# GT = X^T phi(K) in five pieces of 512 columns and a turned strip of 128, with the last two head groups of kv formed later

## The chip, the cores and the metric

One core of one Trainium2 chip runs the whole kernel. The metric is the device time of one execution in microseconds; before the change its median over three runs is 724.76 us (724.48 to 725.0). The kernel's products run on TensorE (PE in the profile, PEld for its weight loads), sums and low halves on VectorE (DVE), copies, high halves and activations on ScalarE (ACT); SyncE (SP) and GpSimd (POOL) issue nearly all DMAs.

## The reference

The input x has 2048 rows of 640. A linear attention block with 32 heads of 20 and a gated linear unit of width 1536 are mixed by a gate:

```python
qkv = x @ wqkv                      # q, k, v: 32 heads of 20
phi = lambda t: where(t > 0, t + 1, exp(t)) + 1e-6
kv  = einsum("bhsd,bhse->bhde", phi(k), v)
z   = einsum("bhsd->bhd", phi(k))
o   = einsum("bhqd,bhde->bhqe", phi(q), kv) / (einsum("bhqd,bhd->bhq", phi(q), z) + 1e-6)
a   = o @ wo
b   = (sigmoid(x @ w_gate) * (x @ w_up)) @ w_down
g   = sigmoid((x * gate_w).sum(-1))
out = g * a + (1 - g) * b
```

All in float32.

## The kernel before

**Precision.** A product in float32 is made of three in a faster format (fp32r): each operand is split into a high and a low half, and `mm3` (lines 406 to 412) issues high x high, high x low and low x high. The split itself (`split`, line 437) is a copy on ScalarE for the high half and a subtraction on VectorE for the low half; names end in h and l. So an operand is ready for its second product only when VectorE has made its low half.

**Stage 1, GT.** V is never formed. Instead the kernel sums GT = X^T phi(K), 640 x 640, over the 16 token tiles of 128 (`GTBatch`, line 978), in five batches: of 2 tiles, three of 4, and 2. A batch has ten pieces, u = 0 to 9: piece u = 2m + h is the block of 128 rows m and of 320 columns h. Each piece gathers its tiles in one PSUM bank (three products a tile) and is then added to `gt` in SBUF by VectorE (in the first batch, copied, some of them by ScalarE). The stationary operand is a block of 128 columns of x (XN), the moving one 320 columns of phi(K) (PK). Between the batches stand the K projections of the next tokens. The eight PSUM banks have four names, ch, dd, cc and rot, with two banks each in turn. Lines 1161 to 1195 run batches 1 to 3, lines 1197 to 1210 the last one (`glast`); its last four sums are put off to the start of the next stage (`p1_tail`).

**Stage 2, the q phase.** `q_phase` (line 2178) has 16 steps for the second half of the tokens: j = 0 and 1 are steps 1 and 2 of a block A (units 2 and 3 of q by a scheme with seven products, s1 to s7), j = 2 and 3 two whole units of q, j = 4 and 5 steps 1 and 2 of a block B (units 0 and 1), j = 6 to 10 steps 3 to 7 of A, j = 11 to 15 those of B. In step 2 of a block VectorE adds the bank dd to c11, in step 5 ScalarE copies ch to c22 and VectorE adds cc to it. Between the steps a table of lists, `extra[j]` (lines 2430 to 2444), puts the small products of the attention, head group by head group (six groups, called parts 0 to 5 below, of 120, 120 and four times 100 columns):

- `kv_part` (line 1573) multiplies a part's columns of `gt` with wv (five plain float32 products, line 1578), and VectorE masks the result to the heads' blocks and splits it (kvt, kvh, kvl). Parts 0 to 5 stand at j = 1, 1, 3, 6, 6, 8.
- `m_part` (line 1589) multiplies a part's kvh, kvl with woh, wol, the halves of that part's rows of wo: two banks, three products of 320 columns each; the second and fifth product read wol. ScalarE copies the results out (ms). Parts 0 to 5 stand at j = 5, 6, 8, 10, 12, 13. The split of wo (`wo_split`, line 1561) is queued two parts ahead; it frees a tile for the load of a further part.

**What sets the order.** Every engine runs its instructions in the order in which the program lists them. The class `Order` makes this list: it keeps a clock for TensorE, ScalarE and VectorE by rough costs, and one for the DMA queues, and `fill` (line 116) puts queued work (splits, sums) on ScalarE and VectorE when by these clocks it is ready and does not make them late. `need(key)` (line 189) puts a queued item at once, ready or not, because a product that reads it comes next. A queued split of wo counts as ready when its load has landed by the planner's clock (line 1571). After stage 1 that clock of SyncE's queue is set forward to the last landing of a DMA that GpSimd issued:

```python
    sp.t = max(sp.t, gp.cell[0])          # line 1508
    load_w()
```

and behind it stand the loads of the raw weights (`wst`), of wv and of wo. `sp.t` and `gp.cell` belong to the planner alone; no instruction comes of them.

Of the kernel before, what the change touches and what calls it, by code (L numbers as in the profile page):

```python
# [7 lines left out]
F32 = mybir.dt.float32  # L8
F32R = mybir.dt.float32r
AF = mybir.ActivationFunctionType  # L10
# [360 lines left out]
def v_cost(w):  # L371
    return 0.07 + w / 960

@with_exitstack
def gated_mix_kernel(ctx: ExitStack, tc: tile.TileContext, xt, xn, wk, wv, wo, wst_q, wst_f, out_t):
# [30 lines left out]
    def mm3(out, l_hi, l_lo, r_hi, r_lo, first, last):  # L406
        nc.tensor.matmul(out, l_hi, r_hi, start=first, stop=False, skip_group_check=True)  # L407
        nc.tensor.matmul(out, l_hi, r_lo, start=False, stop=False, skip_group_check=True)  # L408
        nc.tensor.matmul(out, l_lo, r_hi, start=False, stop=last, skip_group_check=True)  # L409
# [8 lines left out]
    def act(out, src, fn, after="", **kw):  # L418
        order.on_act(width(out), after, out, src)
        nc.scalar.activation(out, src, fn, **kw)  # L420
# [44 lines left out]
    fac_dram = dram.tile([P, NG, P], F32, name="fac_dram")  # L465
    z_dram = dram.tile([P // H, H, DH], F32, name="z_dram")
    m_dram = dram.tile([D, D], F32, name="m_dram")
    mr_dram = dram.tile([P, KC, D], F32, name="mr_dram")
    bdn = HPG * DH

# [12 lines left out]
    def m1_tile(tag, name, dt=F32, rows=P):  # L483
        return m1.tile([rows, D], dt, name=name, tag=tag, bufs=2 if tag == "ma" else 3)
# [489 lines left out]
    def queue_split(b):  # L974
        for s in range(2):
            order.add(a_cost(D), v_cost(D), lambda s=s: k_split(tok(b, s)), ("pk", b))

    class GTBatch:
        def __init__(self, n, blocks):
            self.n, self.tiles = n, [tok(b, s) for b in blocks for s in range(2)]  # L980
            self.ps = {}

        def part(self, u, t0, t1, tag="rot", out=True):
            m, h = divmod(u, 2)
            cs = slice(h * HALF, (h + 1) * HALF)
            ms = slice(m * P, (m + 1) * P)
            if u not in self.ps:
                self.ps[u] = ps_tile(tag)
            ps = self.ps[u][:, :HALF]
            for n in range(t0, t1):  # L990
                i = self.tiles[n]
                mm3(ps, XN[i][0][:, ms], XN[i][1][:, ms], PK[i][0][:, cs], PK[i][1][:, cs],
                    n == 0, n == len(self.tiles) - 1)
            if t1 == len(self.tiles) and out:
                self.out(u)

        def out(self, u):
            m, h = divmod(u, 2)
            ps, dst = self.ps[u][:, :HALF], gt[:, m, h * HALF:(h + 1) * HALF]
            if self.n == 0 and u < 4:  # L1000
# [78 lines left out]
    queue_xn(1)  # L1079
    g = GTBatch(0, [0])  # L1080
    order.slack(True)
    for u in range(2 * KC):
        g.part(u, 0, 2, "rot" if u % 2 else "dd")
        order.fill()
    order.slack(False)
# [2 lines left out]
    for c in range(1, 4):  # L1088
        ck = chunks[c]
        if c == 1:  # L1090
            queue_qw(2)
        a, b = KBlock(2 * c), KBlock(2 * c + 1)
        for n in range(1, 6):
            order.need((ck, n))
            if c == 1 and n >= 3:
                order.need(("ks", (1, 0, 2)[n - 3]))
            getattr(a, f"s{n}")()
            getattr(b, f"s{n}")()
            for _ in range(({1: 1, 2: 1, 3: 1, 5: 1}, {3: 2, 4: 2, 5: 2})[c - 2].get(n, 0) if c > 1 else 0):
# [12 lines left out]
        a.s6()  # L1112
        a.s7()
        a.sum_b()
        a.phi_a()
        b.s6()
        a.phi_b()
        order.need(("pk", 2 * c - 1))
        k_split(tok(2 * c, 0))
        b.s7()  # L1120
        b.sum_b()
        k_split(tok(2 * c, 1))
        if c == 3:
# [46 lines left out]
        for u in range(6 if c == 1 else 4):  # L1170
            g.part(u, 0, 2, ("rot", "dd", "ch", "cc")[u % 4])
# [16 lines left out]
        for u in range(2 * KC):  # L1188
            g.part(u, 2 if u in g.ps else 0, len(g.tiles),
                   ("rot", "dd", "rot", "cc")[u % 4] if c == 3 or u < 8 else "rot")  # L1190
            order.fill()
            if u in (3, 5, 7, 9,):
                order.run("qw")
            if c == 2 and u == 9:
                queue_ls()
    order.need(("xn", 7))
    glast = GTBatch(4, [7])
    tags = ["rot", "rot", "ch", "ch", "dd", "dd", "cc", "cc", "rot", "rot"]

    for u in range(4):  # L1200
        glast.part(u, 0, 2, tags[u])
    for u in range(4, 10):
        glast.part(u, 0, 2, tags[u], out=False)
        order.fill()
        if u == 5:
            wg_split(("q", 1, KC - 1), w_stage)
        elif u == 8:
            glast.out(4)
            glast.out(5)
    p1_tail = [lambda u=u: glast.out(u) for u in range(6, 10)]  # L1210
    p1_cm.__exit__(None, None, None)

    pw_cm = tc.tile_pool(name="pw", bufs=1, side="right", reuse_waits="tile")
# [1793 lines left out]
```

## Time and profile before

| | |
|---|---|
| median of three runs | 724.76 us |
| the profiled execution: span from the first to the last instruction | 722.5 us |
| TensorE busy, share of the span | 718.2 us, 99% |
| VectorE, ScalarE, GpSimd busy | 587.1, 370.0, 114.0 us |
| granted TensorE clock | 1.000 |
| stage 1, last GT product to the q phase | 140.99 us from the span's start |
| products of GT | 480, of 320 columns |

The profile gives the span of one execution and not its own time on the clock of the runs; the median lies 2.26 us above the span. A line of a timeline gives start, duration, engine, line of the program, operation, what it writes and reads, and the shapes; in brackets stand the idle time of the engine before it and what ended it. TensorE's products are pipelined: their durations overlap, and the time that one takes in a stream is the distance from start to start.

### The profile page before, as it was taken

How to read it: one execution, taken by the hardware profiler on the slowest of the kernel's cores; microseconds unless marked ns; L12 is line 12 of the kernel's file. 1: busy time of each engine (PE TensorE's matmuls, PEld its weight loads, DVE VectorE, ACT ScalarE, POOL GpSimd, SP SyncE). 2: the span in 40 equal slices, each digit the busy share in tenths (PEclk: the TensorE clock that was granted, in tenths of full speed). 3: DMA queues.
4: the chain of work that ended last, by engine and by line, in shares of the span. 5: the costliest groups of instructions: out<-in, count | busy, mean ns of one | idle time of the engine just before them, and what ended most of it. 6: DMA issues, size and time to landing. Idle time of an engine off the chain costs nothing.

```text
span 722.5 us, 10190 instructions
## 1 busy us (share of the span) xinstructions
PE 718.2 (99%) x3539; PEld 616.7 (85%) x3539; DVE 587.1 (81%) x1028; ACT 370.0 (51%) x686; POOL 114.0 (16%) x184
## 2 busy tenths in 40 slices
PE   9999999999999999999999999999999999999998
PEld 8999999988888888888888888888888888888886
DVE  6898888988677989898989977447696968799895
ACT  6884748367556654545364664354423242454451
POOL 0211112113311212111210224001010101002200
PEclk9999999999999999999999999999999999999999
DMA  7677689598787866757687899968989895959947
GB/s 258 162 230 182 179 196 286 129 357 280 273 303 259 325 241 234 262 221 264 244 321 273 255 313 360 404 222 292 364 256 309 247 395 182 407 217 332 217 101 240
DMA packets 81690, 191.31 MB, mean 265 GB/s; under 512 B 12154, under 2 KB 40202, under 8 KB 77926
## 3 DMA queue, kind: packets, MB, share of 16 engines
q1 hardware_dynamic: 60726, 117.72, 49.6%
q0 software_dynamic: 20624, 72.70, 30.2%
q8 instruction: 28, 0.46, 0.3%
q10 hardware_dynamic: 288, 0.23, 0.1%
q14 instruction: 24, 0.20, 0.1%
HBM read 113.14 MB, written 75.20 MB: 261 GB/s over the span
## 4 chain that ended last, share of the span: by engine, by line
PE 99%; DMA 0%; DVE 0%; ACT 0%; issue 0%
PE ch L407 11%; PE ch L409 11%; PE ch L408 11%; PE cc L409 9%; PE cc L407 9%; PE cc L408 9%; PE dd L407 7%; PE dd L408 7%; PE dd L409 7%; PE rot L407 5%; PE rot L408 5%; PE rot L409 5%; PE rot L1578 1%; PE dd L2735 1%; PE ch L2735 0%; DMA xnh<-wk 0%
## 5 line engine op out<-in xcount | busy, mean ns | idle before, releaser
L420 ACT ACTIVATE c<-ch 128x512 f32<-128x512 f32 x54 | 32.3, 597 | 84.2 <-PE ch L409 83.4
L424 DVE TENSOR_TENSOR hf<-c,hf 128x512 fp32r<-128x512 f32 x80 | 54.4, 687 | 19.3 <-ACT hf L420 18.9
L420 ACT ACTIVATE hf<-c 128x512 fp32r<-128x512 f32 x80 | 48.9, 624 | 31.1 <-DVE c L424 31.0
L424 DVE TENSOR_TENSOR c<-cc,c 128x512 f32<-128x512 f32 x42 | 28.9, 688 | 28.3 <-PE cc L409 17.4
L407 PE MATMUL ch<-xth,ws 128*128 128x512 f32 x112 | 43.6, 389 | 0.0
L408 PE MATMUL ch<-xtl,ws 128*128 128x512 f32 x112 | 43.6, 389 | 0.0
L409 PE MATMUL ch<-xth,ws 128*128 128x512 f32 x112 | 43.6, 389 | 0.0
L424 DVE TENSOR_TENSOR c<-c,c 128x512 f32<-128x512 f32 x52 | 35.7, 687 | 3.3 <-ACT c L420 2.7
L424 DVE TENSOR_TENSOR tb<-rot,tb 128x512 f32<-128x512 f32 x56 | 36.1, 682 | 0.3 <-PE rot L409 0.3
L407 PE MATMUL dd<-xrh,wg 128*128 128x512 f32 x90 | 35.2, 391 | 0.0
L408 PE MATMUL dd<-xrl,wg 128*128 128x512 f32 x90 | 35.1, 390 | 0.0
L409 PE MATMUL dd<-xrh,wg 128*128 128x512 f32 x90 | 35.0, 389 | 0.0
L420 ACT ACTIVATE c<-dd 128x512 f32<-128x512 f32 x22 | 13.1, 596 | 41.4 <-PE dd L409 41.4
L407 PE MATMUL cc<-xbh,ws 128*128 128x512 f32 x84 | 32.7, 389 | 0.0
L408 PE MATMUL cc<-xbl,ws 128*128 128x512 f32 x84 | 32.7, 389 | 0.0
L409 PE MATMUL cc<-xbh,ws 128*128 128x512 f32 x84 | 32.7, 389 | 0.0
L424 DVE TENSOR_TENSOR tb<-dd,tb 128x512 f32<-128x512 f32 x36 | 24.7, 686 | 9.3 <-PE dd L409 9.2
L420 ACT ACTIVATE dd<-ch 128x512 f32<-128x512 f32 x22 | 12.8, 582 | 35.9 <-PE ch L409 35.9
L424 DVE TENSOR_TENSOR tb<-cc,tb 128x512 f32<-128x512 f32 x36 | 24.5, 684 | 1.9 <-PE cc L409 1.9
L424 DVE TENSOR_TENSOR wst<-wst 128x256 f32<-128x256 f32 (+1 forms) x65 | 24.6, 396 | 1.4
L409 PEld LDWEIGHTS ch<-xth,ws 128*128 128x128 f32 x112 | 21.0, 188 | 4.7 <-DVE ws L424 0.3
L408 PEld LDWEIGHTS ch<-xtl,ws 128*128 128x128 f32 x112 | 21.0, 188 | 4.3
(703 smaller groups left out, 2378.9 us busy)
## 6 DMA issues: line engine op xcount, KB each, us to landing
wf<-ws POOLq DMA_DIRECT2D x12, 1152.0 KB, 7.5
ws<-wf SPq DMA_DIRECT2D x11, 1152.0 KB, 8.8
wst<-wst_f SPq DMA_DIRECT2D x12, 640.0 KB, 4.9
wf<-wg POOLq DMA_DIRECT2D x12, 640.0 KB, 6.1
wd<-wd POOLq DMA_DIRECT2D x12, 640.0 KB, 8.1
wg<-wf SPq DMA_DIRECT2D x12, 640.0 KB, 6.9
wf<-wd SPq DMA_DIRECT2D x10, 640.0 KB, 11.0
xnst<-xn SPq DMA_DIRECT2D x16, 320.0 KB, 4.5
```

Source lines behind the costliest of these rows:

```text
L407: nc.tensor.matmul(out, l_hi, r_hi, start=first, stop=False, skip_group_check=True)
L408: nc.tensor.matmul(out, l_hi, r_lo, start=False, stop=False, skip_group_check=True)
L409: nc.tensor.matmul(out, l_lo, r_hi, start=False, stop=last, skip_group_check=True)
L420: nc.scalar.activation(out, src, fn, **kw)
L424: nc.vector.tensor_tensor(out, a, b, op=op)
L1578: nc.tensor.matmul(ps[:w, :w], v[:, m, :w], gt[:, m, c0:c0 + w], start=(m == 0), stop=(m == KC - 1))
L2735: nc.tensor.matmul(ps, l, r, start=new, stop=j == 1 and k == ks[-1], skip_group_check=True)
```

## The change

A GT batch now has seven pieces instead of ten. Pieces 0 to 4 hold 128 rows of GT each and its first 512 columns: the same stationary operands, 512 moving columns. The last 128 columns of GT are made transposed: now the 128 columns of PK are stationary and x moves, in two pieces of 384 and 256 columns (`STRIP`). They gather in the same place of `gt`, columns 512 to 640, but there element (r, m, c) is GT's element (m 128 + c, 512 + r). In the last batch the two strip pieces come first; then VectorE transposes the strip within blocks of 32 x 32 into a tile `turned`, GpSimd's queue stores it in DRAM and fetches it back in four DMAs with the blocks exchanged, and ScalarE copies it into `gt` (`gt_back`, at the end of step j = 8). Head groups 4 and 5 reach into these columns; their kv parts move from j = 6 and 8 to j = 9 and 10. `GTBatch.part`, `out` and the loops over pieces follow; lines from 986 on are shifted by 30 in the end.

```diff
+    STRIP = {KC: (0, 3), KC + 1: (3, KC)}
+    def gt_turn():
+        turned = m1_tile("mb", "turned")
+        order.on_vec(D, "", 1.0, turned, gt[:, :, TG:])
+        nc.vector.transpose(turned.rearrange("p (b m c) -> p m b c", m=KC, c=H),
+                            gt[:, :, TG:].rearrange("p m (b c) -> p m b c", c=H))
+        gp.dma_start(gt_dram, turned)
+        back = m1_tile("mb", "back")
+        src = gt_dram.rearrange("(a r) (b n) -> b r a n", r=H, b=P // H)
+        for b in range(P // H):
+            gp.dma_start(back[b * H:(b + 1) * H].rearrange("r (a n) -> r a n", a=P // H), src[b])
+        BACK.append(back)
+    def gt_back():
+        act(gt[:, :, TG:].rearrange("p m (a c) -> p a m c", c=H),
+            BACK[0].rearrange("p (a m c) -> p a m c", m=KC, c=H), AF.Copy)
...
-            ps = self.ps[u][:, :HALF]
             for n in range(t0, t1):
-                i = self.tiles[n]
-                mm3(ps, XN[i][0][:, ms], XN[i][1][:, ms], PK[i][0][:, cs], PK[i][1][:, cs],
-                    n == 0, n == len(self.tiles) - 1)
+                x, pk = XN[self.tiles[n]], PK[self.tiles[n]]
+                if u < KC:
+                    ms = slice(u * P, (u + 1) * P)
+                    ps, l, r = self.ps[u], [t[:, ms] for t in x], [t[:, :TG] for t in pk]
+                else:
+                    b0, b1 = STRIP[u]
+                    ps = self.ps[u][:, :(b1 - b0) * P]
+                    l, r = [t[:, TG:D] for t in pk], [t[:, b0 * P:b1 * P] for t in x]
+                mm3(ps, *l, *r, n == 0, n == len(self.tiles) - 1)
...
-    for u in range(4):
+    for u in (KC, KC + 1, 0):
         glast.part(u, 0, 2, tags[u])
-    for u in range(4, 10):
+    order.add(0, v_cost(D), gt_turn, "turned", first=True)
+    for u in range(1, KC):
         glast.part(u, 0, 2, tags[u], out=False)
         order.fill()
...
-    for hg, (j, t) in enumerate(((1, "rot"), (1, "rot"), (3, "cc"), (6, "rot"), (6, "rot"), (8, "rot"))):
+    for hg, (j, t) in enumerate(((1, "rot"), (1, "rot"), (3, "cc"), (6, "rot"), (9, "rot"), (10, "rot"))):
         extra[j].append(lambda hg=hg, t=t: kv_part(hg, t))
+    extra[8].append(gt_back)
```

The planner then lists the work of VectorE and ScalarE in another order. Numbers behind a name tell buffers apart. VectorE in the q phase before, from the low half of wo's part 1 (wol_1966; that of part 0 stands earlier) to the sum of block B's step 2 (c11_2003):

```order
L424 TENSOR_TENSOR wol_1966<-wo_sb_1841,woh_1965 120x640
L424 TENSOR_TENSOR xz_1528<-xz_1528 128x512
L424 TENSOR_TENSOR xtl_1521<-xst_89,xth_1520 128x2x256
L424 TENSOR_TENSOR xtl_1521<-xz_1528,xth_1520 128x2x256
L424 TENSOR_TENSOR kvt_1984<-cc0_1978,bd_65 100x100
L855 CAST kvh_1987<-kvt_1984 100x100
L424 TENSOR_TENSOR kvl_1988<-kvt_1984,kvh_1987 100x100
L428 SCALAR_TENSOR_TENSOR qe_1964<-qe_1964,qr_1976 128x512
L424 TENSOR_TENSOR ws_2004<-wst_1826,ws_2004 128x640
L424 TENSOR_TENSOR ws_2004<-wst_1826,ws_2004 128x512
L424 TENSOR_TENSOR c11_2003<-dd0_1996,c11_2003 128x512
```

VectorE at the same place after, from the sum of block B's step 2 (c11_1817) through the low halves of wo's parts 0, 1 and 2 (wol_1837, wol_1873, wol_1928), with the sum of A's step 5 (c22_1918) among them:

```order
L424 TENSOR_TENSOR c11_1817<-dd0_1810,c11_1817 128x512
L424 TENSOR_TENSOR wol_1837<-wo_sb_1665,woh_1836 120x640
L424 TENSOR_TENSOR xtl_1414<-xz_1421,xth_1413 128x2x256
L424 TENSOR_TENSOR ws_1848<-wst_1654,ws_1848 128x640
L424 TENSOR_TENSOR ws_1848<-wst_1654,ws_1848 128x512
L424 TENSOR_TENSOR wol_1873<-wo_sb_1669,woh_1872 120x640
L428 SCALAR_TENSOR_TENSOR qe_1879<-qe_1879,c11_1686 128x512
L424 TENSOR_TENSOR kvt_1902<-rot1_1896,bd_65 100x100
L856 CAST kvh_1904<-kvt_1902 100x100
L424 TENSOR_TENSOR kvl_1905<-kvt_1902,kvh_1904 100x100
L424 TENSOR_TENSOR c22_1918<-cc0_1908,c22_1918 128x512
L424 TENSOR_TENSOR wol_1928<-wo_sb_1840,woh_1927 100x640
```

Before, the low halves of wo's parts 0 and 1 stood ahead of the sum of B's step 2; now both stand behind it, and that of part 2 stands behind the sum of A's step 5.

ScalarE around step 5 of A before (its copy of that step is c22_2107; woh_2074 is wo's part 3, part 2 stands earlier, ms_2116 are m's results of part 2):

```order
L420 ACTIVATE ms_2053<-dd0_2061 120x320
L420 ACTIVATE woh_2074<-wo_sb_1969 100x640
L420 ACTIVATE c22_2107<-ch1_1851 128x512
L420 ACTIVATE wg_2121<-wst_2021 128x640
L420 ACTIVATE ms_2116<-dd1_2117 100x320
L420 ACTIVATE ms_2116<-dd0_2127 100x320
L420 ACTIVATE qe_2154<-c22_2107 128x512
```

and after (the copy of step 5 is c22_1918; woh_1927 and woh_1945 are wo's parts 2 and 3, ms_1933 m's results of part 2, gt_86<-back_1629 the copy of the strip):

```order
L420 ACTIVATE c22_1918<-ch1_1678 128x512
L420 ACTIVATE woh_1927<-wo_sb_1840 100x640
L420 ACTIVATE ms_1933<-dd1_1934 100x320
L420 ACTIVATE wg_1943<-wst_1856 128x640
L420 ACTIVATE woh_1945<-wo_sb_1876 100x640
L420 ACTIVATE ms_1933<-dd0_1939 100x320
L420 ACTIVATE gt_86<-back_1629 128x4x5x32
L420 ACTIVATE qe_1966<-c22_1918 128x512
```

The high halves of parts 2 and 3 have moved from ahead of step 5's copy to behind it, and the strip's copy stands behind them all. On SyncE the load of wo's part 2, which the split of part 0 frees, moved behind the load of the last part of wv. TensorE's list has 144 products less; its order changes for the pieces of GT and for parts 4 and 5 of kv.

More of the change, by code (lines that the diff above doesn't have):

```diff
@@ L467, in gated_mix_kernel @@
     m_dram = dram.tile([D, D], F32, name="m_dram")
+    gt_dram = dram.tile([P, D], F32, name="gt_dram")
     mr_dram = dram.tile([P, KC, D], F32, name="mr_dram")
@@ L976, in queue_split @@
             order.add(a_cost(D), v_cost(D), lambda s=s: k_split(tok(b, s)), ("pk", b))
+    STRIP = {KC: (0, 3), KC + 1: (3, KC)}
+    NU = KC + 2
+    def gt_turn():
[9 more added lines that the diff above has]
+        BACK.append(back)
+    BACK = []
+    def gt_back():
+        act(gt[:, :, TG:].rearrange("p m (a c) -> p a m c", c=H),
+            BACK[0].rearrange("p (a m c) -> p a m c", m=KC, c=H), AF.Copy)
     class GTBatch:
@@ L983, in part @@
         def part(self, u, t0, t1, tag="rot", out=True):
-            m, h = divmod(u, 2)
-            cs = slice(h * HALF, (h + 1) * HALF)
-            ms = slice(m * P, (m + 1) * P)
             if u not in self.ps:
                 self.ps[u] = ps_tile(tag)
-            ps = self.ps[u][:, :HALF]
             for n in range(t0, t1):
-                i = self.tiles[n]
-                mm3(ps, XN[i][0][:, ms], XN[i][1][:, ms], PK[i][0][:, cs], PK[i][1][:, cs],
-                    n == 0, n == len(self.tiles) - 1)
+                x, pk = XN[self.tiles[n]], PK[self.tiles[n]]
[7 more added lines that the diff above has]
+                mm3(ps, *l, *r, n == 0, n == len(self.tiles) - 1)
             if t1 == len(self.tiles) and out:
@@ L997, in out @@
         def out(self, u):
-            m, h = divmod(u, 2)
-            ps, dst = self.ps[u][:, :HALF], gt[:, m, h * HALF:(h + 1) * HALF]
-            if self.n == 0 and u < 4:
+            if u < KC:
+                ps, dst = self.ps[u], gt[:, u, :TG]
+            else:
+                b0, b1 = STRIP[u]
+                ps = self.ps[u][:, :(b1 - b0) * P].rearrange("p (m c) -> p m c", c=P)
+                dst = gt[:, b0:b1, TG:]
+            if self.n == 0 and u in (0, 1, KC + 1):
                 vec_copy(dst, ps, "p")
@@ L1081, in gated_mix_kernel @@
     order.slack(True)
-    for u in range(2 * KC):
+    for u in range(NU):
         g.part(u, 0, 2, "rot" if u % 2 else "dd")
@@ L1169, in gated_mix_kernel @@
             queue_xn(7)
-        for u in range(6 if c == 1 else 4):
-            g.part(u, 0, 2, ("rot", "dd", "ch", "cc")[u % 4])
+        first = 4 if c == 1 else 3
+        for u in range(first):
+            g.part(u, 0, 2, ("rot", "dd", "ch", "cc")[u])
             if c == 1 and u == 0:
@@ L1187, in gated_mix_kernel @@
             queue_forms(nx)
-        for u in range(2 * KC):
-            g.part(u, 2 if u in g.ps else 0, len(g.tiles),
-                   ("rot", "dd", "rot", "cc")[u % 4] if c == 3 or u < 8 else "rot")
+        for u in range(NU):
+            g.part(u, 2 if u in g.ps else 0, len(g.tiles), ("rot", "dd", "ch", "cc", "dd", "rot", "rot")[u])
             order.fill()
-            if u in (3, 5, 7, 9,):
+            if u in (2, 3, 4, 6):
                 order.run("qw")
-            if c == 2 and u == 9:
+            if c == 2 and u == NU - 1:
                 queue_ls()
@@ L1197, in gated_mix_kernel @@
     glast = GTBatch(4, [7])
-    tags = ["rot", "rot", "ch", "ch", "dd", "dd", "cc", "cc", "rot", "rot"]
-    for u in range(4):
+    tags = ["ch", "dd", "dd", "cc", "cc", "rot", "ch"]
+    for u in (KC, KC + 1, 0):
         glast.part(u, 0, 2, tags[u])
-    for u in range(4, 10):
+    order.add(0, v_cost(D), gt_turn, "turned", first=True)
+    for u in range(1, KC):
         glast.part(u, 0, 2, tags[u], out=False)
         order.fill()
-        if u == 5:
+        if u == 1:
             wg_split(("q", 1, KC - 1), w_stage)
[L1207 to L1210, printed above, removed]
+        elif u == 3:
+            glast.out(1)
+    p1_tail = [lambda u=u: glast.out(u) for u in range(2, KC)] + [lambda: order.need("turned")]
     p1_cm.__exit__(None, None, None)
```

## The prediction

> **What bounds the kernel now.** I read the page first, then the waits of TensorE, then three timelines (TensorE, VectorE, ScalarE) from the end of the GT products through the first q phase, and last the landings of the loads there.
>
> From the page, the span, the busy times and the chain that ended last:
>
> ```profile
> span 722.5 us, 10190 instructions
> PE 718.2 (99%) x3539; PEld 616.7 (85%) x3539; DVE 587.1 (81%) x1028; ACT 370.0 (51%) x686; POOL 114.0 (16%) x184
> ...
> PE 99%; DMA 0%; DVE 0%; ACT 0%; issue 0%
> ```
>
> From the waits of TensorE, the whole answer (who waited for whom, total, times, longest):
>
> ```profile
> PE rot L496 <- PEq L2998: 0.8, 1, 0.8
> PE ch L1022 <- DVE k1h L855: 0.2, 1, 0.2
> ```
>
> TensorE is the bound from end to end: after the start it never waits. So whatever shortens its products shortens the kernel by as much, whatever makes it wait lengthens the kernel by as much, and no slack further on takes a wait back. The median of 724.76 us is 2.26 us above this execution's span; I take that rest as unchanged and add differences to the median. 0.2% of it, 1.45 us, is about what a measurement of this kernel can tell from no change.
>
> **Part 1: fewer products for GT.** TensorE's timeline gives the start-to-start time of a product at two widths (start, duration, first and next group):
>
> ```profile
> 121.58 0.30 PE L407 MATMUL rot<-pkh,xnh 128*128 128x320 f32 x1
> ...
> 140.99 0.39 PE L407 MATMUL ch<-xah,wg 128*128 128x512 f32 x1
> ...
> 144.42 2.26 PE L1578 MATMUL rot<-gt,wv_sb 128*120 128x120 f32 x20
> 146.44 0.48 PE L407 MATMUL dd<-xrh,wg 128*128 128x512 f32 x1
> 149.94 0.39 PE L407 MATMUL rot<-xbh,wg 128*128 128x512 f32 x1
> ...
> 153.34 1.04 PE L1578 MATMUL cc<-gt,wv_sb 128*100 128x100 f32 x10
> ```
>
> From 121.58 to 140.99 stand 11 pieces of 12 products of 320 columns: 19.41 us / 132 = 147.0 ns. From 149.94 to 153.34 stand 15 products of 512 columns: 226.7 ns. The line through both leaves 14 ns a product beside 0.415 ns a column; it gives 173.6 ns at 384 columns and 120.4 ns at 256. The weight load could set a floor for the narrow ones; but the 20 products from 144.42 to 146.44 (2.02 us) stand 101 ns apart, less than 120.4. GT before is 16 token tiles x 30 products = 480 x 147.0 = 70.6 us. After, it is 240 x 226.7 + 48 x 173.6 + 48 x 120.4 = 68.5 us. The columns are the same; 144 products go. **Gain 2.0 us.**
>
> The Trainium skill, "TensorE: Matmul & The Clock Gate", section "Back-to-back issue gap", gives the isolated gap of a warm matmul as columns over 2.4 GHz plus 2.5 ns. By that figure 144 products less would save an estimated 0.4 us; the rows show 14 ns where it has 2.5, so the measurement decides.
>
> The GT sums on VectorE and ScalarE change from 320 to 512 columns and get fewer; TensorE has two or more pieces between using a PSUM bank and using it again, and in the trace it never waited for one. I cost them at nothing.
>
> **Part 2: the strip's way back.** VectorE gets one transposition (835 ns in the row below, the same amount of data), GpSimd's queue five DMAs, ScalarE one copy of 128x640. The nearest rows for the way through DRAM are z's store and reload (instructions on both, and landings of the DMAs):
>
> ```profile
> L1542 DVE STREAM_TRANSPOSE zturn<-zperm x1: 835/835/835, 184.6 to 184.6; 128x640 f32<-128x640 f32 x1
> ...
> DMA to landing us min/median/max: 4.0/4.6/9.2
> ```
>
> With 4 to 9.2 us each way the strip is back within 20 us of its transposition, which ends before GT does (140.99 above); the copy stands behind A's step 5 (166.05 below), so the landing costs nothing. What waits behind those DMAs on GpSimd is q's first store; nobody waits for that soon.
>
> **Part 3: what moves with it.** This decides. The planner lets the SyncE clock start from the last landing on GpSimd's queue (line 1508), and that is now the strip's return. So it believes the loads of wo later than before, and the order of VectorE and ScalarE shows the splitting of wo (woh on ScalarE, wol on VectorE) pushed back until a product needs it. In the trace of before the splits run ahead. VectorE's timeline (start, duration):
>
> ```profile
> 149.97 0.82 DVE L424 TENSOR_TENSOR wol<-wo_sb,woh 120x640 fp32r<-120x640 f32 x1
> 150.70 1.08 DVE L424 TENSOR_TENSOR wst<-wst 128x256 f32<-128x256 f32 x3
> 151.70 0.69 DVE L424 TENSOR_TENSOR xst<-xst 128x512 f32<-128x512 f32 x1
> 152.30 0.69 DVE L428 SCALAR_TENSOR_TENSOR qe<-qe,qr 128x512 f32<-128x512 f32 x1
> 152.90 0.82 DVE L424 TENSOR_TENSOR wol<-wo_sb,woh 120x640 fp32r<-120x640 f32 x1
> 153.64 0.69 DVE L424 TENSOR_TENSOR xz<-xz 128x512 f32<-128x512 f32 x1
> ...
> 155.64 0.26 DVE L424 TENSOR_TENSOR kvt<-cc,bd 100x100 f32<-100x100 f32 x1
> ...
> 156.35 0.69 DVE L428 SCALAR_TENSOR_TENSOR qe<-qe,qr 128x512 f32<-128x512 f32 x1
> 156.96 1.42 DVE L424 TENSOR_TENSOR ws<-wst,ws 128x640 fp32r<-128x640 f32 x2
> 158.29 0.69 DVE L424 TENSOR_TENSOR c<-dd,c 128x512 f32<-128x512 f32 x1
> ```
>
> and ScalarE's:
>
> ```profile
> 150.19 0.60 ACT L420 ACTIVATE qe<-dd 128x512 f32<-128x512 f32 x1 [2.92 <-PE dd L409]
> 150.69 0.59 ACT L420 ACTIVATE qr<-dd 128x512 f32<-128x512 f32 x1
> ...
> 159.07 0.73 ACT L420 ACTIVATE woh<-wo_sb 100x640 fp32r<-100x640 f32 x1
> ...
> 166.25 0.60 ACT L420 ACTIVATE c<-ch 128x512 f32<-128x512 f32 x1 [3.06 <-PE ch L409]
> 166.74 0.73 ACT L420 ACTIVATE wg<-wst 128x640 fp32r<-128x640 f32 x1
> 167.37 0.76 ACT L420 ACTIVATE ms<-dd 100x320 f32<-100x320 f32 x2
> ```
>
> and TensorE's at the products with wo (m products; the rows of parts 0, 1 and 2 and what follows each):
>
> ```profile
> 157.66 0.31 PE L407 MATMUL cc<-woh,kvh 120*120 120x320 f32 x1
> 158.54 0.40 PE L407 MATMUL ch<-xth,ws 128*128 128x512 f32 x1
> 159.93 0.31 PE L407 MATMUL dd<-woh,kvh 120*120 120x320 f32 x1
> ...
> 166.05 0.31 PE L407 MATMUL dd<-woh,kvh 100*100 100x320 f32 x1
> ```
>
> Before, wol of part 0 is done at 150.79 and of part 1 at 153.72, 4 us ahead of 157.66. Steps from start to start: 0.60 us for 512 columns on VectorE, 0.74 for a wol, 1.00 for three sums of wst, 0.71 for a kv's three steps, 1.33 for both ws; 0.49 on ScalarE for 512 columns, 0.63 for 640, 0.38 for an ms. A unit of q that TensorE ends at 149.94 has its second ScalarE result at 151.28, 1.34 us later. All times below are on the clock of before, less the 2.0 us gained.
>
> *Part 0, behind B's step 2.* The new order on VectorE puts c11, the sum that needs B's last product of step 2, ahead of wol of part 0, which the second m product needs. TensorE ends step 2 at 157.66 - 2.0 = 155.66. VectorE is later still: q's second unit ends at 151.34, its qe can start at 152.7; then kv's steps, three wst, xst, xz (3.5 us) and the xtl that waits for ScalarE's xth (156.4); c11 at 157.0, wol 157.6 to 158.4. The product stands from 155.81 to 158.5: **2.7 us lost**. Were VectorE idle, it would be 0.2 + 0.60 + 0.82 + 0.1 - 0.15 = 1.6.
>
> *Part 1.* m ends at 159.2, A's step 3 (1.39 us) at 160.6. VectorE runs xtl and ws (1.9 us) to 160.3; woh of part 1 stands on ScalarE behind both ms copies (159.8), ends 160.55, wol 161.4. **0.7 us lost**; 0 if ScalarE is quicker.
>
> *Part 2, behind A's step 5.* ScalarE first copies c22 (starts 0.20 after the product, as at 166.25), then splits woh: done 1.42 us after step 5. VectorE adds c22 (0.85 to 1.45), then wol to 2.32. The second m product would have gone at 0.15 and goes at 2.4: **2.25 us lost**, with no backlog in it.
>
> *Part 4 of kv.* It now needs the strip's copy. On ScalarE that stands behind ms, wg, the next woh and ms: from 2.9 after step 5, 0.38 + 0.63 + 0.63 + 0.38 + 0.73 make 5.7. TensorE is there at 3.14 (end of m) + 2.05 (nine products) = 5.2. **0.5 us lost**; 0 to 0.6.
>
> Sum: -2.0 + 2.7 + 0.7 + 2.25 + 0.5 = +4.15, and 724.76 + 4.15 = **728.9 us**. Lower bound of the waits 1.6 + 0 + 2.25 + 0 = 3.85, which gives 726.6. For the upper one there are the loads. SyncE's queue may fetch a further part of wo only when a split has freed a tile, so these loads go out late too. Their landings are bounded by the first two of these rows, of wo's own tile and of wv's; the third is that of the raw weights in this stretch:
>
> ```profile
> DMA to landing us min/median/max: 4.5/4.5/4.5
> ...
> DMA to landing us min/median/max: 4.8/7.6/10.3
> ...
> wst<-wst_f SPq DMA_DIRECT2D x3, 640.0 KB, 6.6
> ```
>
> Part 2's load goes out at 158.4. A's step 5 ends at 166.05 - 2.0, less 0.8 for kv's part 4 that has moved, plus the 3.4 lost so far, 166.6; the load is wanted 0.69 later, at 167.3: at 10.3 us it is 1.4 late. Part 4's goes out near 169 and is wanted such that 10.3 us would cost another 1.3. Nearest is wo's own 4.5, which costs nothing; both together give 731.6. The next raw weights (wst) now stand behind part 2's load on SyncE, go out at 158.5 and land 6.6 later, at 165.1; ScalarE's wg wants them near 170, so they cost nothing.
>
> **The rivals.**
> (a) *VectorE and ScalarE keep up*, only the chains themselves count: 726.6. For it: they have pauses once TensorE waits. Against: VectorE is still behind at 158.29 before, 0.6 us after its product. 0.15.
> (b) *Late loads of wo*: 730.3 to 731.6. For it: 10.3 us occurs in this stretch. Against: the wo row has 4.5. 0.14.
> (c) *Faster: the waits are hidden and only the 2.0 us remain*, 722.8. It would need wol of part 0 ready at 155.8 and of part 2 at step 5's end, that is the splits in effect ahead of c11 and c22; it decides when all waits together stay under 0.55 us. For it: the trace of before, where they were ready. Against: the order. 0.05.
> (d) *About the same*: only part 2's wait is paid, 724.76 - 2.0 + 2.25 = 725.0. 0.07.
> (e) *The gain is not there*, the 14 ns being no fixed cost, and the waits are: 724.76 + 6.15 = 730.9. The 2.5 ns of the Trainium skill's section named above would put this case at an estimated 730.5. Against it stand the three widths. 0.04.
>
> **How the numbers follow.** My forecast has 0.55, with 727.4 to 730.3 as its own range (half a microsecond either way on each of three waits, added up). The range 726.0 to 731.6 takes in (a), (b) and (e) and leaves out (c), (d) and little else. Slower by over 0.2% (above 726.2): forecast, (a), (b) and (e), 0.88. Within: (d), 0.07. Faster: 0.05.
>
> **What would show it.** Right: TensorE's waits, nearly empty before, name wol, woh and gt in the q phase, some 6 us together; products of GT 227 ns apart; GT's stretch 2 us shorter. wol of part 0 starts behind c11 and TensorE's second m product right after it. Wrong: no gap at the m products, or gaps in the GT batches, or a TensorE wait on the strip's landing, or a gap at the first kv part.

## The result, and the profile after

The changed kernel takes **732.58 us** (four runs, 731.82 to 733.62) against 724.62 us before (four runs): ratio 1.0112, 95% interval 1.0098 to 1.0126. It is slower by 7.96 us; the forecast was 4.15 us slower, and 732.58 lies above the end of its range, 731.6.

The profiled execution after, from the page: span, busy times, and the chain that ended last by engine.

```profile
span 730.8 us, 9904 instructions
PE 721.4 (99%) x3395; PEld 606.7 (83%) x3395; DVE 587.5 (80%) x1016; ACT 371.1 (51%) x685; POOL 116.8 (16%) x189
PE 98%; DVE 1%; ACT 1%; issue 0%; DVEq 0%
```

The span is 8.3 us longer. TensorE has 144 products fewer, and yet is busy 3.2 us longer; the rest is idle time. Its waits, the whole answer but for the start:

```profile
PE dd L407 <- ACT woh L420: 2.1, 2, 1.3
PE cc L407 <- ACT woh L420: 1.2, 1, 1.2
PE cc L408 <- DVE wol L424: 1.0, 1, 1.0
PE dd L408 <- DVE wol L424: 0.9, 2, 0.5
```

All 5.2 us are waits for the halves of wo, none for the strip. Where the time lies is seen from two places in TensorE's timeline: the first product of the q phase and the first behind it. After, then before:

```profile
140.50 0.39 PE L407 MATMUL ch<-xah,wg 128*128 128x512 f32 x1
...
191.51 0.40 PE L407 MATMUL ch<-xah,wg 128*128 128x512 f32 x1
```

```profile
183.61 0.39 PE L407 MATMUL ch<-xah,wg 128*128 128x512 f32 x1
```

Before, the first of them stood at 140.99. So stage 1 is only 0.49 us shorter, and the q phase takes 51.01 us instead of 42.62: 8.39 us more. Behind it nothing of weight happens. TensorE's timeline after, at the products with wo of parts 0, 1 and 2, and behind part 2:

```profile
156.92 0.39 PE L409 MATMUL dd<-xrh,wg 128*128 128x512 f32 x1
158.50 0.41 PE L407 MATMUL cc<-woh,kvh 120*120 120x320 f32 x1 [1.19 <-ACT woh L420]
159.93 0.41 PE L408 MATMUL cc<-wol,kvh 120*120 120x320 f32 x1 [1.03 <-DVE wol L424]
160.17 0.31 PE L409 MATMUL cc<-woh,kvl 120*120 120x320 f32 x1
...
161.92 0.40 PE L409 MATMUL ch<-xth,ws 128*128 128x512 f32 x1
163.10 0.41 PE L407 MATMUL dd<-woh,kvh 120*120 120x320 f32 x1 [0.78 <-ACT woh L420]
163.96 0.41 PE L408 MATMUL dd<-wol,kvh 120*120 120x320 f32 x1 [0.45 <-DVE wol L424]
164.20 0.31 PE L409 MATMUL dd<-woh,kvl 120*120 120x320 f32 x1
...
168.91 0.39 PE L409 MATMUL ch<-xth,ws 128*128 128x512 f32 x1
170.61 0.39 PE L407 MATMUL dd<-woh,kvh 100*100 100x320 f32 x1 [1.31 <-ACT woh L420]
171.47 0.39 PE L408 MATMUL dd<-wol,kvh 100*100 100x320 f32 x1 [0.47 <-DVE wol L424]
171.70 0.31 PE L409 MATMUL dd<-woh,kvl 100*100 100x320 f32 x1
...
172.58 0.63 PE L408 MATMUL ch<-xtl,wu 128*128 128x512 f32 x1
...
175.14 0.63 PE L408 MATMUL ch<-xrl,wu 128*128 128x512 f32 x1
```

A loss is read from starts, not from the brackets: from 156.92 to 160.17 pass 3.25 us where three products without a wait take 0.227 + 2 x 0.147 = 0.52. So the waits cost 2.73 us at part 0, and in the same way 2.28 - 0.52 = 1.76 at part 1 and 2.79 - 0.52 = 2.27 at part 2: 6.76 in all. The last two rows show something new: six products take 2.56 us, 427 ns each instead of 227. The windows of TensorE say why (stretches of 3.41 us, the length of the one with the lower clock, counted from its start; start and end, length, busy time and instructions, granted clock, DMA share, GB/s):

```profile
155.36:158.77 3.41, 2.22 (x10) 1.00 1.05 399
158.77:162.18 3.41, 2.38 (x12) 1.00 0.71 213
162.18:165.60 3.42, 2.19 (x17) 1.00 0.95 378
...
169.01:172.42 3.41, 1.63 (x9) 1.00 0.65 208
172.42:175.84 3.42, 3.42 (x10) 0.50 0.39 89
```

From 172.42 on the granted clock is 0.50 for one window of 3.41 us. The products from 172.28 to 175.93 take 1.60 us more for it. 6.76 + 1.60 = 8.36, nearly the whole of the q phase's 8.39.

Stage 1: a piece of GT after, two of its products thirteen steps apart on TensorE's timeline:

```profile
85.09 0.39 PE L407 MATMUL rot<-pkh,xnh 128*128 128x512 f32 x1
...
88.11 0.40 PE L408 MATMUL ch<-pkl,xnh 128*128 128x512 f32 x1
```

3.02 us / 13 = 232 ns; over all 240 such products the distances average 231.9 ns, where those of the q phase have 227. The strip's two pieces in a batch of four tiles, 12 products of 384 columns, 12 of 256, and what follows:

```profile
61.41 0.34 PE L407 MATMUL rot<-xnh,pkh 128*128 128x384 f32 x1
...
63.53 0.28 PE L407 MATMUL rot<-xnh,pkh 128*128 128x256 f32 x1
...
64.93 0.31 PE L407 MATMUL ch<-k1h,xah 128*128 128x322 f32 x1
```

Over all 48 of each, the distances average 175.0 and 118.6 ns. So GT takes 69.75 us instead of 70.52: a gain of 0.77. The other products of stage 1, with the start, came out 0.28 us longer.

### The profile page after: what moved, and what is told of

It reads as the page before. It is cut to its first block, busy times and chain, and to the rows that moved or that the text cites. A ratio compares the mean times of both kernels' runs of the same rounds, so it can differ in the third digit from the quotient of the medians.

```text
span 730.8 us, 9904 instructions
## 1 busy us (share of the span) xinstructions
PE 721.4 (99%) x3395; PEld 606.7 (83%) x3395; DVE 587.5 (80%) x1016; ACT 371.1 (51%) x685; POOL 116.8 (16%) x189
## 4 chain that ended last, share of the span: by engine, by line
PE 98%; DVE 1%; ACT 1%; issue 0%; DVEq 0%
PE ch L408 11%; PE ch L407 11%; PE ch L409 11%; PE cc L407 9%; PE cc L409 9%; PE cc L408 9%; PE dd L408 7%; PE dd L409 7%; PE dd L407 7%; PE rot L407 5%; PE rot L409 5%; PE rot L408 5%; PE rot L1608 1%; PE dd L2766 1%; PE rot L497 0%; PE ch L2766 0%
```

## The experiments

Two theories to begin with. *Late splits*: the planner's clock for the loads, moved by the strip's return, sets the late order of wo's splits, and that order alone makes the gaps and with them the half clock. *Strip and kv*: the strip's way back and the late parts of kv load the queues and VectorE.

**1. The planner's clock kept.**

```
+        cell = gp.cell
         gp.dma_start(gt_dram, turned)
...
+        gp.cell = cell
         BACK.append(back)
```

> The changed kernel with one thing undone: the strip's way back no longer moves the planner's clock for the loads, so that the splits of wo stand early again; GT in five pieces and a strip, its return through DRAM and the late parts of kv stay. Theory (late splits): in the changed kernel TensorE stood still 2.7, 1.8 and 2.3 us at the products with wo of parts 0, 1 and 2, and after the third of these gaps its clock was granted at half for 3.4 us, another 1.6 to 1.7 us; GT itself gained 0.8 and the start lost 0.3. So all of the waits and the half clock go, and what is left is 724.6 - 0.8 + 0.3 = 724.1 us (723.6 to 725.0). Rival (the strip's return or the late parts of kv make the waits, by load on the queues or by data that comes late): the gaps stay in part, above 727. Rival (GT gains the forecast 2.0 us and the profile hid it): 722.7.

Measured 726.94 us, ratio 1.0041 (1.0028 to 1.0053). TensorE's waits:

```profile
PE dd L407 <- DVE ms L856: 1.1, 1, 1.1
...
PE dd L407 <- DVE c L424: 0.7, 1, 0.7
PE cc L407 <- DVE c L424: 0.5, 1, 0.5
```

No wait for woh or wol is left, the profiled execution has no half clock (one of the five runs, of 728.85 us, has a mean granted clock of 0.997), and 5.6 of the 7.96 us are gone. But three new gaps have come, all behind VectorE: by starts 0.96 us at part 1 (the bank of c11's sum), 1.31 at part 5 and 0.74 at a cc bank. In the changed kernel VectorE caught up while TensorE stood still: its longest pauses in the q phase, 3.27 and 2.35 us, come after the gaps at parts 1 and 2. The forecast of 724.1 failed: the first theory holds for the bulk, and 2.4 us above before are left to the second.

**2. The late clock put into the kernel before.**

```
-    sp.t = max(sp.t, gp.cell[0])
+    sp.t = max(sp.t, order.pe + 7.66)
```

> The kernel before with one line altered: the planner's clock for the loads starts 7.5 us later, as the strip's return makes it in the changed kernel; GT in its old pieces, no strip, kv at its old places. Theory (late splits): the order of the splits is that of the changed kernel, so the same three gaps of 6.8 us in all, and about one window of half clock of 1.7 us, follow without anything of the strip: 724.6 + 6.8 + 1.7 = 733.1 us (731.4 with no half clock, 734.8 with two). Rival (the strip and the late kv are needed for the waits): within 2 us of before, under 727.

Measured 732.08 us, ratio 1.0114 (1.0099 to 1.0130): 7.5 us, of one altered number that issues no instruction. All four waits are those of the changed kernel, shown above, to the tenth. The windows are different; they are laid by the half clock that the trace shows behind the last product, from 728.57 us on, in steps of 3.41 us back. The emptiest of the q phase and the one behind the third gap:

```profile
158.54:161.96 3.42, 1.96 (x10) 1.00 0.26 78
...
172.20:175.61 3.41, 2.94 (x21) 1.00 0.24 75
```

That settles the bulk. With the same gaps the profiled execution kept the full clock: no window of the q phase had TensorE busy for less than 1.96 of 3.42 us (57%), where 1.63 (48%) stood ahead of the half clock in the changed kernel. The windows lie where they lie; the gaps fell into them otherwise.

**3. The gaps filled.** Products of constants ahead of the waiting ones.

```
             ps = ps_tile(tag)
+            for _ in range((11, 7, 9, 0, 0, 0)[hg] if h == 0 else 0):
+                nc.tensor.matmul(ps, warm[:, :P], warm, start=True, stop=True)
```

> The changed kernel with idle products: ahead of the products with wo of parts 0, 1 and 2 stand 11, 7 and 9 products of constants (512 columns, some 0.22 us each) into the bank that the next product overwrites, so TensorE waits the same but is busy in the gaps; nothing else differs. Theory (the half clock is a cost of its own, brought on by the gaps): the gaps are as long, the granted clock is 1.000 throughout, and 1.6 to 1.7 us go: 730.9 us. Rival (the half clock comes by something else than idleness, or the slow products hide behind another wait): 732.6, or up to 1 us more where the idle products overrun.

Measured 732.16 us (731.87 to 732.36), ratio 1.0107 (1.0093 to 1.0120). The half clock is gone from the q phase, and the runs spread over 0.5 us instead of 1.8, but hardly any time is won. Two new waits, of the sort found in experiment 1, took its place:

```profile
PE cc L407 <- DVE c L424: 0.4, 1, 0.4
PE rot L1608 <- ACT gt L420: 0.2, 1, 0.2
```

By starts they cost 0.70 and 0.47 us. The second is the wait for the strip's copy, forecast at 0.5 and absent from the changed kernel only because the half clock brought TensorE there later. So the half clock costs 1.6 us where it falls, and net at most some 0.4, which the intervals don't separate from nothing.

**4. GT's operands exchanged**, in the kernel of experiment 1.

```
-                    ps, l, r = self.ps[u], [t[:, ms] for t in x], [t[:, :TG] for t in pk]
+                    ps, l, r = self.ps[u], [t[:, ms] for t in pk], [t[:, :TG] for t in x]
```

> The kernel with the kept clock, and in GT's five wide pieces the two operands exchanged: 128 columns of phi(K) stand still and 512 columns of x move. This leaves the wide part of GT turned, so what is computed from it is not the reference's; number and widths of all products are the same. In the changed kernel GT's 512-column products stood 231.9 ns apart where those of the later stages stand 227. Theory (the moving rows of phi(K) cost the 5 ns): 227 ns, 240 products give 1.2 us less than the kernel with the kept clock, 722.9. Rival (the place in the program, not the operand): 232 ns as before and no difference, 724.1.

Thirteen steps on TensorE's timeline:

```profile
85.13 0.40 PE L408 MATMUL ch<-xnl,pkh 128*128 128x512 f32 x1
...
88.17 0.39 PE L409 MATMUL dd<-xnh,pkl 128*128 128x512 f32 x1
```

3.04 us / 13 = 234 ns, 232.9 over all: no gain, so the operand that moves isn't the cause. The time, 729.37 us (1.0069, 1.0055 to 1.0083), is not comparable, since the planner ordered VectorE's and ScalarE's work otherwise. Its q phase shows the clock again:

```profile
180.42:183.83 3.41, 1.39 (x8) 1.00 0.41 133
183.83:187.24 3.41, 3.41 (x11) 0.50 0.73 239
```

**5. kv early again.** The strip's reload lands by 154 us, so experiment 1's kernel can copy it at j = 4 and form kv's last parts where they stood before.

```
-    for hg, (j, t) in enumerate(((1, "rot"), (1, "rot"), (3, "cc"), (6, "rot"), (9, "rot"), (10, "rot"))):
+    for hg, (j, t) in enumerate(((1, "rot"), (1, "rot"), (3, "cc"), (6, "rot"), (6, "rot"), (8, "rot"))):
         extra[j].append(lambda hg=hg, t=t: kv_part(hg, t))
-    extra[8].append(gt_back)
+    extra[4].append(gt_back)
```

> The kernel with the kept clock, and kv's last two parts back at their old places (j = 6 and 8), the strip's copy at j = 4: in the traces its reload has landed by 154 us, and part 4 wants it at 160. With the kept clock alone three gaps were left: 0.96 us at the products with wo of part 1 (the bank of c11's sum), 1.31 at those of part 5 (the bank that VectorE copies out for part 4), 0.74 at a cc bank in B's step 6. Theory (late kv: its six steps, 1.4 us of VectorE, stand in front of those last two): they go, the first stays: 726.9 - 1.31 - 0.74 = 724.9 us (724.2 to 725.6). Rival (VectorE is late by the work behind GT alone, and the backlog shows elsewhere): no gain, 726.5 to 727.

Measured 725.11 us, ratio 1.0010 (1.0001 to 1.0020), as forecast. The wait for ms at part 5 is gone; the one at part 1 stayed (0.96 by starts) and, against the expectation, also the one at the cc bank (0.68):

```profile
PE dd L407 <- DVE c L424: 0.7, 1, 0.7
PE cc L407 <- DVE c L424: 0.4, 1, 0.4
```

**6. kv late in the kernel before.**

```
-    for hg, (j, t) in enumerate(((1, "rot"), (1, "rot"), (3, "cc"), (6, "rot"), (6, "rot"), (8, "rot"))):
+    for hg, (j, t) in enumerate(((1, "rot"), (1, "rot"), (3, "cc"), (6, "rot"), (9, "rot"), (10, "rot"))):
```

> The kernel before with one thing added: kv's last two parts at j = 9 and 10 as in the changed kernel; no strip, GT in its old pieces, the clock for the loads as before. Theory (late kv costs by itself): about 2.0 us by VectorE's late copies and sums, 726.6 us. Rival (it costs only where VectorE leaves GT some 1.7 us later, as it does in the changed kernel): 724.6 to 725.0.

Measured 725.72 us, ratio 1.0017 (1.0008 to 1.0026): 1.1 us, between the two. One gap, 1.03 by starts, at part 5:

```profile
PE dd L407 <- DVE ms L855: 0.8, 1, 0.8
```

So late kv costs 1.1 us by itself, and 1.8 (experiment 1 less experiment 5, which also moved the strip's copy) where VectorE leaves GT late.

**7. Part 4's copies on ScalarE**, in the kernel of experiment 1 (no part has the number 9).

```
-            if hg == 4:
+            if hg == 9:
                 vec_copy(ms[:w, cs], ps[:w, :HALF], "p")
```

> The kernel with the kept clock, and the two copies of the products with wo of part 4 on ScalarE, as those of the other parts, and not on VectorE. Theory (the 1.31 us at part 5 are VectorE's backlog): that gap goes, and VectorE has 0.88 us less to do ahead of the cc bank, so that most of the 0.74 goes too: 725.0 us (724.7 to 725.7). Rival (ScalarE is as late there): 726.9 as with the kept clock.

Measured 726.96 us, ratio 1.0034 (1.0022 to 1.0047): the rival, by the time. ScalarE frees the bank late as well, though less so (0.3 us instead of 1.1, the row below), the wait at the cc bank stays at 0.5 us, and in the profiled execution a load of wv came 0.5 us late:

```profile
PE dd L407 <- ACT ms L420: 0.3, 1, 0.3
```

**8. Other banks**, in the kernel of experiment 5; the first line pair is that of the products with wo, the second kv's.

```
-    for hg, (j, t) in enumerate(((5, "cc"), (6, "dd"), (8, "dd"), (10, "dd"), (12, "dd"), (13, "dd"))):
+    for hg, (j, t) in enumerate(((5, "cc"), (6, "rot"), (8, "dd"), (10, "dd"), (12, "dd"), (13, "dd"))):
...
-    for hg, (j, t) in enumerate(((1, "rot"), (1, "rot"), (3, "cc"), (6, "rot"), (6, "rot"), (8, "rot"))):
+    for hg, (j, t) in enumerate(((1, "rot"), (1, "rot"), (3, "cc"), (6, "dd"), (6, "dd"), (8, "rot"))):
```

> The kernel with the kept clock and the early kv, and the banks exchanged: the products with wo of part 1 go to rot, which has long been read, and kv's parts 3 and 4 to dd. Theory (the 0.96 us left at part 1 are the wait for c11's bank and for nothing else): that gap goes as well, and what is left is what GT gained, 724.6 - 0.8 + 0.3 = 724.1 us (723.5 to 724.6). Rival (VectorE is late with whatever comes next, so the wait moves on to kv's parts or to the sum c22): 724.9 or more.

Measured 726.04 us, ratio 1.0021 (1.0011 to 1.0030). The gap at part 1 vanished and came back, twice as long, at part 5:

```profile
PE dd L407 <- DVE ms L856: 1.7, 1, 1.7
```

That fits a VectorE that is late, so that whoever needs it next waits, and not a matter of one bank.

**9. The strip unturned**, in the kernel of experiment 5.

```
...
-        nc.vector.transpose(turned.rearrange("p (b m c) -> p m b c", m=KC, c=H),
-                            gt[:, :, TG:].rearrange("p m (b c) -> p m b c", c=H))
...
-        gp.dma_start(gt_dram, turned)
+        gp.dma_start(gt_dram.rearrange("p (m c) -> p m c", m=KC), gt[:, :, TG:])
```

> The kernel with the kept clock and the early kv, without the strip's transposition on VectorE: the strip goes to DRAM as it is, in rows of 128, and comes back through the same DMAs, so the last 128 columns of GT are wrong and what is computed from them is not the reference's; all else is the same. Theory (the transposition, 0.84 us on VectorE at the end of GT, is on the path, since VectorE then has no pause until the products with wo of part 1): the gap of 0.96 us there shrinks to about 0.2, and the one of 0.68 at the cc bank goes in part: 725.1 - 0.76 = 724.35 us, down to 723.7 if both go. Rival (the transposition lies beside other work, as the prediction had it): 725.1 as before.

Measured 728.28 us, ratio 1.0055 (1.0039 to 1.0071): inconclusive. The planner's order changed, and the store to DRAM, 2.7 us in the changed kernel, took 8.3 by the DMA rows, with all that is queued behind it on GpSimd. The three waits of experiment 1 are there again (by the bracket 1.05, 1.51 and 0.46 us).

**10. Both remedies**: the kernel of experiment 8 with the edit of experiment 7.

> The kernel with the kept clock, the early kv and the exchanged banks, and the two copies of the products with wo of part 4 on ScalarE. With the exchanged banks two gaps were left, 1.94 us at part 5 (the bank that VectorE copies out) and 0.72 at the cc bank. Theory (both are VectorE's backlog, and ScalarE has room): the first goes to ScalarE's time and mostly vanishes, the second halves: 726.0 - 1.9 = 724.1 us (723.7 to 724.8). Rival (ScalarE copies as late, since it waits for VectorE's work itself): 725.2 to 726.0.

Measured 727.04 us (725.71 to 728.44), ratio 1.0043 (1.0030 to 1.0056). A miss: the profiled execution has four short waits in the q phase, three for ScalarE (0.5, 0.3 and 0.2 us) and one for a load of wv (0.3), and the runs spread wide.

**11. The transposition twice**, in the kernel of experiment 5, with nothing else moved.

```
         nc.vector.transpose(turned.rearrange("p (b m c) -> p m b c", m=KC, c=H),
                             gt[:, :, TG:].rearrange("p m (b c) -> p m b c", c=H))
+        nc.vector.transpose(turned.rearrange("p (b m c) -> p m b c", m=KC, c=H),
+                            gt[:, :, TG:].rearrange("p m (b c) -> p m b c", c=H))
```

> The kernel with the kept clock and the early kv, the strip's transposition done twice on VectorE; the order of everything else and the result stay. Theory (the transposition is on the path: VectorE has no pause from the end of GT to the sum c11 that frees the bank of part 1's products): 0.76 us more, 725.1 + 0.76 = 725.9 us (725.6 to 726.6), and the gap at part 1 grows from 0.96 to about 1.7. Rival (it lies beside other work): 725.1, gap unchanged.

Measured 726.34 us, ratio 1.0026 (1.0016 to 1.0036), 1.2 us above the kernel of experiment 5. The gap at part 1 (TensorE's timeline) grew by starts from 0.96 to 1.68:

```profile
160.00 0.31 PE L409 MATMUL dd<-woh,kvl 120*120 120x320 f32 x1
161.73 0.41 PE L407 MATMUL dd<-woh,kvh 120*120 120x320 f32 x1 [1.43 <-DVE c L424]
```

0.76 us more on VectorE at the end of GT is 0.72 us more idle time of TensorE twenty microseconds later: added work there is on the path to part 1. It doesn't account for the 1.2 us of the medians: in this trace the wait at the cc bank, 0.68 us in experiment 5, is gone, and the profiled execution took 725.80 us, where that of experiment 5 took 725.91. Nor is VectorE without a pause on that path; in experiment 5 it stands still ahead of its part of ws, for ScalarE's, which itself waits for VectorE's xtl:

```profile
159.59 0.83 DVE L424 TENSOR_TENSOR ws<-wst,ws 128x640 fp32r<-128x640 f32 x1 [0.81 <-ACT ws L420]
```

**12. A fifth of the transposition**, the rest copied unturned by ScalarE.

```
+        nc.scalar.activation(turned.rearrange("p (m c) -> p m c", m=KC), gt[:, :, TG:], AF.Copy)
         nc.vector.transpose(turned.rearrange("p (b m c) -> p m b c", m=KC, c=H)[:, :1],
-                            gt[:, :, TG:].rearrange("p m (b c) -> p m b c", c=H))
+                            gt[:, :1, TG:].rearrange("p m (b c) -> p m b c", c=H))
```

> The same kernel with only the first 128 of the strip's 640 columns a row transposed on VectorE, while ScalarE, idle there, copies the strip as it is; all DMAs and the order of everything else stay. This leaves most of the strip unturned, so the last 128 columns of GT are wrong and what is computed from them is not the reference's. Theory: some 0.6 us less on VectorE, the gap at part 1 shrinks from 0.96 to about 0.35, 724.5 us (724.0 to 724.9). Rival (beside other work): 725.1, gap unchanged.

Measured 725.51 us, ratio 1.0013 (1.0004 to 1.0021): inconclusive by the time, since in the profiled execution TensorE also waited 0.9 us in stage 1. That wait has nothing to do with the edit: it lies 26 us ahead of ScalarE's new copy. ScalarE's kb stood behind its copy of qraw, for whose load VectorE waited 2.31 us there and 0.31 in experiment 5. TensorE's row, then ScalarE's:

```profile
110.55 0.42 PE L407 MATMUL ch<-k2h,xth 128*128 128x322 f32 x1 [0.89 <-ACT kb L420]
...
136.55 0.74 ACT L986 ACTIVATE turned<-gt 128x640 f32<-128x640 f32 x1 [6.10 <-DVE gt L424]
```

The gap at part 1 can be read: 0.90 us, 0.06 less than in experiment 5, where the theory had 0.35. VectorE was some 0.5 us earlier against TensorE behind GT, but then waited for ScalarE's xth, ahead of which stands the copy of the returned strip (0.63 us from 157.40 on):

```profile
158.69 0.69 DVE L424 TENSOR_TENSOR xtl<-xst,xth 128x512 fp32r<-128x512 f32 x1 [0.17 <-ACT xth L420]
```

So less work on VectorE alone doesn't take this wait away; the chain through ScalarE is close behind.

None of these kernels beats the one before; experiment 5 comes nearest.

## Why the prediction was wrong, and where it was right

**Right: the mechanism, and two of the four waits.** Experiment 2 shows that the late order alone costs 7.5 us, experiment 1 that undoing it takes the waits for woh and wol away. Part 0 was sized at 2.7 and measured 2.73; part 2 at 2.25 and measured 2.27. At part 0 the first product waited as well, 1.19 us for ScalarE's woh, which the forecast did not have; since wol came later still, it added nothing. Rival (b), late loads of wo, did not happen: at part 2 ScalarE's woh starts 0.49 us behind c22, the pace of its work, and waits for no DMA.

**Failed step 1: "Gain 2.0 us", from "14 ns a product beside 0.415 ns a column".** The gain was 0.77. That line was drawn through GT's 320 columns and the q phase's 512, and it is the line of the later stages, where 256 columns take 119.8 ns in the traces. GT's own four widths lie on another: 118.6 ns at 256 columns, 146.9 at 320 (before), 175.0 at 384 and 231.9 at 512 are, to 0.3 ns, 5.2 ns a product beside 0.443 ns a column. 144 x 5.2 ns = 0.75 us, which is what was gained. The two lines cross near 320 columns, the one width of GT that the prediction had, so nothing warned of the second. Rival (e), "the 14 ns being no fixed cost", was right in direction and, for most of the 14 ns, in its reason. (The 132 products behind the 147.0 ns are six pieces of 12 and ten of 6, not eleven of 12; the distance holds.) Why GT's columns are dearer stays open: experiment 4 rules out the moving operand, and in the changed kernel's trace the products of 512 columns that fall into busy time of VectorE and ScalarE average 231.6 ns, those beside neither 232.1.

**Failed step 2, a term left out: the clock.** The sum took the granted clock of before, 1.000, over into a kernel with 6 us of gaps. Behind the third gap came a window of half clock that cost 1.60 us, and with the gaps filled (experiment 3) it stayed away. The Trainium skill, "TensorE: Matmul & The Clock Gate", section "What's actually happening", has the clock set by how busy TensorE was in a free-running window of 3413 ns; the trace agrees (3.41 us at 0.50). The same page, in "HAM oscillation", warns of gaps above about 3.4 us. Here the longest was 1.31 us by the bracket, and the measurement decides: what went with the half clock was the window's busy share. In the q phases of all traces, windows of 48% and 41% have half clock after them, those of 56% (experiment 9) and more have none. One window at the very end of experiment 6's kernel has 46% and no half clock in the window behind it, so the limit itself is not settled:

```profile
719.15:722.57 3.42, 1.58 (x14) 1.00 0.34 107
```

**Failed step 3: part 1, "0.7 us lost", measured 1.76.** "woh of part 1 stands on ScalarE behind both ms copies" left out what stands ahead of these on ScalarE, the two ws that wait for VectorE's xtl; ScalarE's timeline after:

```profile
160.51 1.26 ACT L420 ACTIVATE ws<-wst 128x640 fp32r<-128x640 f32 x2 [1.55 <-DVE xtl L424]
161.68 0.74 ACT L420 ACTIVATE ms<-cc 120x320 f32<-120x320 f32 x2
162.31 0.73 ACT L420 ACTIVATE woh<-wo_sb 120x640 fp32r<-120x640 f32 x1
```

They take 1.17 us from start to start; with them the forecast would have been about 1.9. The prediction followed VectorE's queue all through, and ScalarE's only from the ms copies on.

**Failed step 4: part 4 of kv, "0.5 us lost", measured 0.** Experiment 3 shows it at 0.47 once TensorE runs at full clock; in the changed kernel the half clock hid it.

**Failed step 5, without effect on this sum: part 2 of the working, the strip's way back.** That the landing "costs nothing" held. The transposition and the copy on ScalarE stand there without a price, and once the large waits are gone both lie on or close to the path: a second transposition lengthened the gap at part 1 by 0.72 us (experiment 11), and with four fifths of it gone ScalarE, behind the strip's copy, held it at 0.90 (experiment 12). "TensorE is the bound from end to end" was true of before, and VectorE had little room behind it: the first theory's 724.1 for experiment 1 rested on that same step and missed by 2.8 us.

The sum by the measured terms: -0.77 + 0.28 + 2.73 + 1.76 + 2.27 + 0 + 1.60 = +7.87; the starts behind the q phase lie 7.90 us apart.

## What to carry to other kernels

A number that only a planner reads can cost more than the instructions that moved it: when a change adds a transfer, look for every clock that takes its landing as a start, and read the orders of all engines of the chain, not only of the one that is waited for. When an estimate puts gaps of some microseconds into the engine that was never idle, price the clock too, by the busy share of stretches of 3.4 us. Draw a line of prices from widths of the stretch that it is meant for: here a line through two stretches made 2.0 us out of 0.77. And where a second engine has little pause behind the first, a wait taken away can come back at the next place that needs that engine (experiments 1 and 8); less work for it helps only as far as the next engine behind it allows (experiment 12).

## What the runs showed of the hardware

- The half clock comes in whole windows (3.41 us at 0.50) and by their place: with equal gaps one execution had one such window in the q phase and one of experiment 2 none. The four runs of the changed kernel had a mean granted clock of 0.995 to 0.998 and spread over 1.8 us; with the gaps filled, 0.5 us.
- In GT's stretch products of 256, 320, 384 and 512 columns stand 118.6, 146.9, 175.0 and 231.9 ns apart, 5.2 ns a product beside 0.443 a column; in the later stages 119.8 at 256, 147 at 320 and 227 at 512. With the operands exchanged the 512 columns take 232.9.
- The strip's store of 320 KB to DRAM landed after 2.7 us in rows of 2560 bytes, and after 8.3 us in rows of 512 bytes (experiment 9). There it also went out right behind another transfer on GpSimd's queue and beside SyncE's first loads of the q phase, so the rows are not shown to be the cause.
